# Attention, two mixture layers and a list scheduler on one core: sums and conversions of the attention stage put in another order and partly on another engine

## Chip, cores and metric

One core of one Trainium2 chip runs the whole program. The metric is the device time of one execution in microseconds; of the kernel before three runs were timed, and their median stands for it.

## The reference

Inputs are q, k and v of shape (4, 12, 448, 64), a cap of 30, and the weights of two layers. Cut to what matters:

```python
scores = cap * np.tanh(scale * q @ k.T / cap)
attn = np.exp(scores - max); attn = attn / attn.sum(-1)
x = (attn @ v).transpose(...).reshape(1792, 768)
# soft mixture of 8 experts with 4 slots each
logits = x @ phi                       # (1792, 32)
d = softmax(logits, over tokens); c = softmax(logits, over slots)
slot_out[e] = relu((d.T @ x)[e] @ w1[e]) @ w2[e]
x = c @ slot_out
# dense layer, 768 -> 2048 -> 768
y = (s * relu(x @ w_in) ** 2 + b) @ w_out
```

## The kernel before

The program has three stages. The **attention stage** goes over 24 pairs of heads (`NP`). Keys are cut into four chunks j = 0 to 3 of a pair n (three of 128 keys for both heads, and one in which the last 64 keys of both heads lie side by side). For each pair TensorE transposes q and k (`emit_tr`, L443), VectorE or ScalarE copies them out of PSUM (`emit_trc`, L410), TensorE makes the scores (`emit_qk`, L486), ScalarE takes tanh (L494) and exp (L508), and TensorE multiplies by v (`emit_av`, L529 and L534), which VectorE or ScalarE copies out to xu (`emit_avc`, L410). The row sums of exp are gathered in a tile es: `emit_es` (L516) adds the chunks 0 and 1, then chunk 2, in two additions over 128 x 896, and `emit_esl` (L521) adds chunk 3 in two additions over 64 x 448. Each two pairs, `emit_den` (L552) sums es over the partitions with a matrix of ones, into four groups of 32 output partitions, one for each head; for the last pair it takes chunks 2 and 3 straight from exp, so those two heads have three matmuls each. Then come the transposed denominators (`emit_row_t`, L565; `emit_rd`, L570 and L574), the logits (`emit_lg`, L580; `emit_lgw`, L588; `emit_lgr`, L597 to L606), the transposed outputs (`emit_xt`, L612; `emit_xtm`, L617), and after each six pairs a running softmax over tokens.

The weights `w_in` and `w_out` reach the program as 64-bit words. Twenty pieces of 768 KB are **converted** to 32-bit floats during the attention stage, where VectorE, GpSimd and ScalarE have room: SyncE loads the words (`cv_load`, L201), VectorE makes two passes (`conv_a`, L214 and L217), ScalarE one (`conv_f`, L224), VectorE or GpSimd adds the two parts (`conv_m`, L227), and SyncE stores the piece to a scratch area (`cv_store`, L334). The words have two buffers, w. SyncE also loads the experts' weights ahead (`load_next`, L356 and L362): ten pieces of w1, four of w2, and after the last conversion six more of w2, in buffers that the conversion had held.

The **expert stage** (L934 to L1003) is fed with the rest of the experts' weights as buffers of the attention stage come free. The **dense stage** (from L1055 on) loads the converted pieces and makes y.

The order of the attention stage isn't written by hand. `ListSchedule.run` takes all operations with an assumed duration on each engine that may do them, their needs, buffers (`acq`, `rel`) and a priority, and plays them forward in an assumed time: it takes the engine that can start first, and there the operation with the smallest priority among those that can start within 0.02. An operation with two engines goes to the one on which it ends first, with an extra charge for some (`DES`, `DESL`, `HACT`). What comes out is an order for each engine; the assumed times are not in the program. On the chip each engine goes through its list in order and waits at an instruction until its inputs are there. A result counts as there `lat` after its operation's end, 0.2 by default. Conversions have the priority `CV0 + CVP * i`, on a scale on which a pair of heads is 2, and none is loaded before `CVA`.

```python
PX, PA, DES, DESL, HACT = -0.32, 1.5, 4.98, 1.5, 0.96
CV0, CVP, CVA, WA = 9.33, 6.53, 20.19, 30.39
...
op(("cl", i), [(SP, 2.19)], cv_load, [], pr - 6, [("w", i)], lat=LAT, after=CVA)
op(("ca", i), [(DVE, 2.0)], cv_a, [("cl", i)], pr, [("cm", i), ("ce", i)], [("w", i)])
```

Of the kernel before, what the change touches and what calls it, by code (L numbers as in the profile page):

```python
# [28 lines left out]
ACT, DVE, POOL, PE, SP = "ACT", "DVE", "POOL", "PE", "SP"  # L29


class ListSchedule:

    def __init__(self, rings):
        self.bufs = rings
        self.ops = {}

    def add(self, name, engs, fn, need=(), prio=0.0, acq=(), rel=(), after=0.0, lat=0.2):

        self.ops[name] = dict(
            engs=engs, fn=fn, need=list(need), prio=prio, acq=acq, rel=rel, after=after, lat=lat
        )

    def run(self):
        end, free, freed, holds = {}, {}, {}, {}
        got = {r: [] for r in self.bufs}
        waits, after = {}, {}  # L50
        for name, o in self.ops.items():
            need = set(o["need"])
            waits[name] = len(need)
            for d in need:
                after.setdefault(d, []).append(name)
            for x in o["rel"]:
                holds[x] = holds.get(x, 0) + 1
        ready = [name for name, n in waits.items() if n == 0]
        while ready:
            best = {}  # L60
            for name in ready:
                o = self.ops[name]
                t = max([o["after"]] + [end[d] for d in o["need"]])
                for ring, _ in o["acq"]:
                    k = len(got[ring]) - self.bufs[ring]
                    if k >= 0:
                        t = max(t, freed.get((ring, got[ring][k]), 1e9))
                if t < 1e8:
                    _, t, eng, dur = min(
                        (max(t, free.get(e, 0.0)) + d + sum(x), max(t, free.get(e, 0.0)), e, d)  # L70
                        for e, d, *x in o["engs"]
                    )
                    best.setdefault(eng, []).append((t, o["prio"], name, dur))
            eng = min(best, key=lambda e: min(c[0] for c in best[e]))
            t0 = min(c[0] for c in best[eng])
            t0, _, name, dur = min((c for c in best[eng] if c[0] <= t0 + 0.02), key=lambda c: c[1])
            ready.remove(name)
            o = self.ops[name]
            free[eng] = t0 + dur
            end[name] = free[eng] + o["lat"]  # L80
            for ring, owner in o["acq"]:
                got[ring].append(owner)
            for x in o["rel"]:
                holds[x] -= 1
                if not holds[x]:
                    freed[x] = end[name]
            o["fn"](eng)
            for d in after.get(name, ()):
                waits[d] -= 1
                if not waits[d]:  # L90
                    ready.append(d)
        assert len(end) == len(self.ops)
# [3 lines left out]
def kernel(  # L96
# [16 lines left out]
    nc = tc.nc  # L113
    B, H, S, D = q.shape
# [25 lines left out]
    for j in range(3):  # L140
        blk = ident[32 * j:32 * j + 32, 32 * j:32 * j + 32]
        nc.scalar.copy(
            out=rep[32 * j:32 * j + 32],
# [142 lines left out]
    def run(safe):  # L286
        W1N, W2N = (4, (4,)) if safe else (10, (4, 6))
        NV, NEB, NEL, NES, NXU, NXQ, NQK = 2, 4, 2, 2, 4, 3, 2
        PX, PA, DES, DESL, HACT = -0.32, 1.5, 4.98, 1.5, 0.96
        CV0, CVP, CVA, WA = 9.33, 6.53, 20.19, 30.39  # L290

        PT, PDEN, PLG, PLW, PXT, PXM, PSO, PSL = -2.67, 1.0, 2.0, 3.4, 3.33, 2.05, 0.25, 4.75
        wctx = ExitStack()
# [76 lines left out]
        ones = c1_p.tile([128, 128], F32, name="ones")  # L370
# [22 lines left out]
        KC = S // 128  # L393
# [4 lines left out]
        spt, et, est, xut = {}, {}, {}, {}  # L398
# [4 lines left out]
        def tp(name):  # L403
            return ps_t.tile([128, 512], F32, tag="tp", name=name)
# [137 lines left out]

        def emit_den(g, _):
            pst["den", g] = ps = tp("dn")
            for j in range(4):
                n, h = 2 * g + j // 2, j % 2
                parts = [(slice(0, 128), est[n][:, h])]
                if n == NP - 1:
                    rows = slice(KL * h, KL * h + KL)
                    parts += [(slice(0, 128), et[n, KC - 1][:, h]), (rows, et[n, KC][rows, 0])]  # L550
                for i, (rows, x) in enumerate(parts):
                    nc.tensor.matmul(  # L552
                        out=ps[32 * j:32 * j + 32, 0:S], lhsT=ones[rows, 0:32], rhs=x,
                        start=(i == 0), stop=(i == len(parts) - 1),
                    )

        def emit_row_c(which, g, e):
            dnt[which, g] = t = sb_p.tile([128, S], F32, tag="dn", name="dn")
# [160 lines left out]
        ))  # L719

        def op(name, engs, f, need=(), prio=0.0, acq=(), rel=(), **kw):
            sch.add(name, engs, lambda e: f(*name[1:], e), need, prio, acq, rel, **kw)

        def cp(dve=True, hact=HACT):
            return [(DVE, 0.62)] * dve + [(ACT, 0.53, hact)]

        LAT = 2.0
        op(("const",), [(SP, 0.1)], load_const, prio=3.0, lat=LAT, after=2.0)
        for n in range(NP):
            f = 2 * n  # L730
            for w in "qk":
                i = ("ld", w, n)
# [3 lines left out]
            i = ("ld", "v", n)  # L736
# [8 lines left out]
            for j in range(KC + 1):  # L745
                u, m = f + j * 2 / (KC + 1), 1 if j < KC else 0.5
# [9 lines left out]
                rel = [(ring, (n, j))]  # L756
                if 0 < j < (KC if n < NP - 1 else KC - 1):
                    op(
                        ("es", n, j), [(POOL, 2.3), (DVE, 1.3, DES)], emit_es,
                        [("exp", n, j), ("exp", n, 0) if j == 1 else ("es", n, j - 1)], u + 1,  # L760
                        [("es", n)] if j == 1 else [], rel + [("e", (n, 0))] * (j == 1),
                    )
                if j == KC and n < NP - 1:
                    for h in range(2):
                        op(
                            ("esl", n, h), [(POOL, 1.2), (DVE, 0.68, DESL)], emit_esl, [("exp", n, j), ("es", n, j - 1)],
                            u + 1, [], rel,
                        )
                op(
                    ("av", n, j), [(PE, 0.85)], emit_av, [("exp", n, j), i] + [("av", n, j - 1)] * (j > 0), u + PA,  # L770
# [4 lines left out]
        for g in range(NQ):  # L775
            bb, gq = divmod(g, NQUAD)
            u0, last = 4 * g + 4, g == NQ - 1
# [3 lines left out]
            if last:  # L781
                es += [("es", NP - 1, KC - 2)] + [("exp", NP - 1, j) for j in (KC - 1, KC)]
                rel += [("e", (NP - 1, KC - 1)), ("el", (NP - 1, KC))]
            op(("den", g), [(PE, 0.82)], emit_den, es, u0 + PDEN, [("tp", ("den", g))], rel)
            if last:
                for j in range(2):
                    sch.add(
# [60 lines left out]
        need = []  # L848
        for i in range(len(cvs)):
            pr = CV0 + CVP * i  # L850
            op(("cl", i), [(SP, 2.19)], cv_load, [], pr - 6, [("w", i)], lat=LAT, after=CVA)
            op(("ca", i), [(DVE, 2.0)], cv_a, [("cl", i)], pr, [("cm", i), ("ce", i)], [("w", i)])
            op(("cf", i), [(ACT, 0.92)], cv_f, [("ca", i)], pr, [], [("w", i)])
            op(("cmul", i), [(DVE, 1.23), (POOL, 1.83)], cv_m, [("cf", i)], pr, [], [("ce", i)])
            op(("cst", i), [(SP, 1.1)], cv_store, [("cmul", i)], pr, [], [("cm", i)], lat=LAT)
            need = [("cst", j) for j in range(i + 1)]

# [488 lines left out]
```

## Time and profile before

| what | value |
|---|---|
| median of 3 runs | 662.75 us (657.78 to 663.97) |
| the profiled execution | 664.11 us |
| its span, first to last instruction | 662.3 us |
| mean granted TensorE clock | 0.959 |
| busy share: TensorE (PE), VectorE (DVE), ScalarE (ACT), GpSimd (POOL) | 92%, 56%, 60%, 30% |
| attention stage, expert stage, dense stage, about | 0 to 306, 306 to 380, 380 to 662 us |
| HBM traffic | 125.14 MB read, 13.37 MB written |

PE is the engine of matmuls, DVE is VectorE, ACT ScalarE, POOL GpSimd, SP SyncE with its DMA queue. A row of a timeline gives the start and the length of an instruction in us and, in brackets, how long its engine had been idle before it and which instruction ended that. In rows by stretch, an engine's number is its busy time in the stretch, in brackets its instructions; PEclk is the granted clock of TensorE (1.00 is 2.4 GHz, the lower level 0.50 is 1.2 GHz). "DMA share" is the mean busy share of the 16 DMA engines; it can read slightly over 1.

### The profile page before, as it was taken

What the parts mean: (1) busy time and instruction counts of PE and PEld (TensorE: products, weight loads), DVE (VectorE), ACT (ScalarE), POOL (GpSimd) and SP (SyncE); (2) the same over time, 40 slices, a digit from 0 to 9 for tenths busy, and PEclk for the clock granted to TensorE, in tenths of its full rate; (3) what the DMA queues carried; (4) which work ended last, traced back from release to release, by engine and by line L of the source; (5) the groups of instructions that cost most, each with busy time, mean ns of one, the idle gap of its engine ahead of it and who ended that gap; (6) DMA issues with size and microseconds to landing.
All of it is one profiled execution on the core that took longest, in us unless ns stands there. A gap on an engine that the chain in (4) does not pass through costs nothing.

```text
span 662.3 us, 10246 instructions
## 1 busy us (share of the span) xinstructions
PE 607.6 (92%) x3994; PEld 361.7 (55%) x3994; DVE 369.0 (56%) x518; ACT 396.5 (60%) x566; POOL 199.6 (30%) x116
## 2 busy tenths in 40 slices
PE   6979989889899999987985689999999999999995
PEld 3323333333233333333652368888888888888784
DVE  2397877768974445335460158992467669611221
ACT  4884876677666775720000188886666666656683
POOL 1694647576755555500000153421000000000000
PEclk9998989899999999996997789999999999999998
DMA  8675998979978531239999997340587779200201
GB/s 153 176 239 164 322 283 276 310 240 294 293 242 254 193 70 29 78 126 345 405 402 405 397 367 254 133 140 1 177 310 255 247 250 328 102 1 1 95 1 53
DMA packets 110345, 139.27 MB, mean 210 GB/s; under 512 B 52432, under 2 KB 84944, under 8 KB 110288
## 3 DMA queue, kind: packets, MB, share of 16 engines
q1 hardware_dynamic: 109344, 138.43, 63.6%
q8 instruction: 33, 0.54, 0.3%
q10 hardware_dynamic: 944, 0.10, 0.1%
q14 instruction: 24, 0.20, 0.1%
HBM read 125.14 MB, written 13.37 MB: 209 GB/s over the span
## 4 chain that ended last, share of the span: by engine, by line
PE 74%; DMA 12%; DVE 9%; ACT 2%; issue 1%; POOL 1%; SPq 0%; DVEq 0%; ACTq 0%; POOLq 0%
PE y L1197 23%; PE y L1198 12%; PE sp L486 10%; PE av L529 8%; DMA w2c<-in_moe_w_dram 5%; PE tr L443 3%; DMA w<-in_moe_w_out_dram 3%; PE av L534 2%; DVE cm L217 2%; PE h1p L946 2%; PE dn L552 2%; DVE cm L214 2%; PE xt L612 2%; PE gp L1129 2%; DMA w<-in_moe_w_in_dram 2%; DMA w<-scr 2%
## 5 line engine op out<-in xcount | busy, mean ns | idle before, releaser
L494 ACT ACTIVATE e<-sp,tsc 128x896 f32<-128x896 f32 x96 | 87.2, 911 | 78.9 <-PE sp L486 77.5
L1197 PE MATMUL y<-wo,gh 128*128 128x512 f32 x336 | 127.0, 400 | 0.0
L1174 DVE TENSOR_TENSOR gl<-r,gh 128x512 fp32r<-128x512 f32 (+1 forms) x65 | 44.5, 685 | 102.3 <-ACT r L1159 102.2
L486 PE MATMUL sp<-qs,ks 64*128 64x448 f32 (+1 forms) x384 | 98.4, 592 | 0.0
L1198 PE MATMUL y<-wo,gh 128*128 128x256 f32 x336 | 94.4, 281 | 0.0
L508 ACT ACTIVATE e<-e,capt 128x896 f32<-128x896 f32 x96 | 89.7, 946 | 1.8
L529 PE MATMUL av<-e,vn 128*64 128x448 f32 x288 | 74.0, 591 | 5.5 <-DVE xu L410 5.5
L516 POOL TENSOR_TENSOR es<-e 128x896 f32<-128x896 f32 x24 | 51.1, 2129 | 88.4 <-ACT e L508 55.0
L1146 ACT ACTIVATE r<-gp 128x512 f32<-128x512 f32 (+1 forms) x65 | 35.0, 539 | 60.8 <-PE gp L1129 59.3
L1197 PEld LDWEIGHTS y<-wo,gh 128*128 128x128 f32 x336 | 63.2, 188 | 13.8 <-issue 1.6
L1197 PE MATMUL y<-wo,gl 128*128 128x512 f32 x168 | 66.7, 397 | 0.0
L1198 PEld LDWEIGHTS y<-wo,gh 128*128 128x128 f32 x336 | 63.1, 188 | 1.7
L268 DVE TENSOR_REDUCE rng<-w 128x1 f32<-128x768 f32 x64 | 56.9, 944 | 0.0
L217 DVE SCALAR_TENSOR_TENSOR cm<-w,cm 128x768 int32<-128x768 int32 x32 | 53.3, 1664 | 1.1
L486 PEld LDWEIGHTS sp<-qs,ks 64*128 64x128 f32 (+1 forms) x384 | 28.1, 178 | 44.4 <-issue 24.1
L521 POOL TENSOR_TENSOR es<-es,e 64x448 f32<-64x448 f32 x35 | 49.3, 1410 | 8.4 <-ACT e L508 6.2
L516 POOL TENSOR_TENSOR es<-es,e 128x896 f32<-128x896 f32 x23 | 50.7, 2206 | 3.7 <-ACT e L508 2.7
L1159 ACT ACTIVATE r<-r,bt,st 128x512 f32<-128x512 f32 (+1 forms) x65 | 49.1, 756 | 1.8
L1159 ACT ACTIVATE gh<-r,bt,st 128x512 fp32r<-128x512 f32 (+1 forms) x65 | 49.1, 757 | 1.6
L1198 PE MATMUL y<-wo,gl 128*128 128x256 f32 x168 | 47.1, 281 | 0.0
L1197 PE MATMUL y<-woe,gh 128*128 128x512 f32 x112 | 44.3, 418 | 0.0
L214 DVE TENSOR_SCALAR cm<-w 128x768 int32<-128x768 int32 x32 | 35.4, 1107 | 15.5 <-DMA w<-in_moe_w_out_dram 8.4
(152 smaller groups left out, 907.8 us busy)
## 6 DMA issues: line engine op xcount, KB each, us to landing
w<-in_moe_w_in_dram SPq DMA_DIRECT2D x32, 768.0 KB, 5.8
w<-in_moe_w_out_dram SPq DMA_DIRECT2D x32, 768.0 KB, 6.1
w1c<-in_moe_w_dram SPq DMA_DIRECT2D x24, 1024.0 KB, 9.5
w2c<-in_moe_w_dram SPq DMA_DIRECT2D x26, 768.0 KB, 12.7
scr<-cm SPq DMA_DIRECT2D x20, 384.0 KB, 5.1
w<-scr SPq DMA_DIRECT2D x20, 384.0 KB, 5.9
qn<-in_q_dram SPq DMA_DIRECT2D x24, 224.0 KB, 4.1
kn<-in_k_dram SPq DMA_DIRECT2D x24, 192.0 KB, 4.3
```

The costliest lines, as they stand in the source:

```text
L214: nc.vector.tensor_scalar(out=m, in0=hi, scalar1=3, scalar2=0x3FFFFFF8, op0=ALU.logical_shift_left, op1=ALU.bitwise_and)
L217: nc.vector.scalar_tensor_tensor(out=m, in0=hi, scalar=-0x40000000, in1=m, op0=ALU.bitwise_and, op1=ALU.bitwise_or)
L268: nc.vector.tensor_reduce(out=rng[:, j, i:i + 1], in_=hi, axis=AX.X, op=o, apply_absolute_value=True)
L486: nc.tensor.matmul(out=sp[:, h, 0:S] if j < KC else sp[KL * h:KL * h + KL, 0, 0:S], lhsT=ks[n][rows, 128 * j:min(128 * j + 128, S)], rhs=q ...
L494: nc.scalar.activation(out=e, in_=spt.pop((n, j))[:, 0:m, 0:S], func=AF.Tanh, scale=tsc)
L508: nc.scalar.activation(out=e, in_=e, func=AF.Exp, scale=capt)
L516: eng.tensor_tensor(out=t, in0=et[n, 0] if j == 1 else t, in1=et[n, j], op=ALU.add)
L521: eng.tensor_tensor(out=t, in0=t, in1=et[n, KC][KL * h:KL * h + KL, 0], op=ALU.add)
L529: nc.tensor.matmul(out=out, lhsT=vt[n][:, KC * h + j, :], rhs=et[n, j][:, h], start=(j == 0), stop=False)
L1159: nc.scalar.activation(out=out, in_=in_, func=AF.Identity, scale=st, bias=bt)
L1197: nc.tensor.matmul(out=ya, lhsT=lhsT, rhs=w[:, 0:512], start=first, stop=last)
L1198: nc.tensor.matmul(out=yb, lhsT=lhsT, rhs=w[:, 512:768], start=False, stop=last and i0 == per - 1)
```

## The change

`ListSchedule` gets a new rule. Operations can be marked with `port=(DVE, POOL)`; among these, one doesn't start in the assumed time before the last marked one on either engine has ended. Marked are the es additions (`es`, `esl`) and the conversion's passes on DVE and POOL (`ca`, `cmul`). The extra charges for DVE fall (`DES` 4.98 to 1.0, `DESL` 1.5 to 0.5, `HACT` 0.96 to 0.5), the assumed durations of the marked operations are shorter, and the default `lat` is 0.6 instead of 0.2 for all of the stage's operations that go through `op` but qk, tanh and exp. Conversion i isn't loaded before `CVA + 9.5 * i`, its words are taken to need 3.0 instead of 2.0 to land, and conversions have an earlier priority (`CVP` 6.53 to 2.0). `emit_den` goes through the parts in the outer loop and the heads in the inner one; the last one's priority is later by 1.

```diff
+        def start(o, e, t):
+            return max(t, free.get(e, 0.0), port[0] if e in o["port"] else 0.0)
...
+            if eng in o["port"]:
+                port[0] = free[eng]
...
-        PX, PA, DES, DESL, HACT = -0.32, 1.5, 4.98, 1.5, 0.96
-        CV0, CVP, CVA, WA = 9.33, 6.53, 20.19, 30.39
+        PX, PA, DES, DESL, HACT = -0.32, 1.5, 1.0, 0.5, 0.5
+        CV0, CVP, CVA, CVT, WA = 9.33, 2.0, 20.19, 9.5, 30.39
+        LATE = 0.6
...
-                for i, (rows, x) in enumerate(parts):
-                    nc.tensor.matmul(
-                        out=ps[32 * j:32 * j + 32, 0:S], lhsT=ones[rows, 0:32], rhs=x,
-                        start=(i == 0), stop=(i == len(parts) - 1),
-                    )
+            for i in range(3):
+                for j in range(4):
+                    if i < len(parts[j]):
+                        rows, x = parts[j][i]
+                        nc.tensor.matmul(
+                            out=ps[32 * j:32 * j + 32, 0:S], lhsT=ones[rows, 0:32], rhs=x,
+                            start=(i == 0), stop=(i == len(parts[j]) - 1),
+                        )
...
+            kw = {"lat": LATE if name[0] not in ("qk", "tanh", "exp") else 0.2, **kw}
...
-                        ("es", n, j), [(POOL, 2.3), (DVE, 1.3, DES)], emit_es,
+                        ("es", n, j), [(POOL, 2.1), (DVE, 1.1, DES)], emit_es,
...
-                            ("esl", n, h), [(POOL, 1.2), (DVE, 0.68, DESL)], emit_esl, [("exp", n, j), ("es", n, j - 1)],
-                            u + 1, [], rel,
+                            ("esl", n, h), [(POOL, 1.13), (DVE, 0.63, DESL)], emit_esl, [("exp", n, j), ("es", n, j - 1)],
+                            u + 1, [], rel, port=BOTH,
...
-            op(("cl", i), [(SP, 2.19)], cv_load, [], pr - 6, [("w", i)], lat=LAT, after=CVA)
-            op(("ca", i), [(DVE, 2.0)], cv_a, [("cl", i)], pr, [("cm", i), ("ce", i)], [("w", i)])
+            op(("cl", i), [(SP, 2.19)], cv_load, [], pr - 6, [("w", i)], lat=3.0, after=CVA + CVT * i)
+            op(("ca", i), [(DVE, 1.55)], cv_a, [("cl", i)], pr, [("cm", i), ("ce", i)], [("w", i)], port=BOTH)
...
-            op(("cmul", i), [(DVE, 1.23), (POOL, 1.83)], cv_m, [("cf", i)], pr, [], [("ce", i)])
+            op(("cmul", i), [(DVE, 0.95), (POOL, 1.63)], cv_m, [("cf", i)], pr, [], [("ce", i)], port=BOTH)
```

The first place is on DVE, around pair 2 of heads. In the order before, L521 is an es addition of chunk 3, L214 and L217 are the conversion's first passes (here of the third piece, w_437), the three L410 copy xu, q and k out of PSUM.

```order
L521 TENSOR_TENSOR es<-es,e 64x448
L214 TENSOR_SCALAR cm<-w_437 128x768
L217 SCALAR_TENSOR_TENSOR cm<-w_437,cm 128x768
L410 COPY xu<-av 128x448
L410 COPY qs<-tr 128x448
L410 COPY ks<-tr 128x448
L588 TENSOR_TENSOR lw<-rowt,rd 112x512
L227 ISA cm<-cm,ce 128x1536
```

In the order now the same place reads (L524 is the es addition over 128 x 896, L529 that over 64 x 448, L418 the copies, L221 and L224 the conversion's passes, now of the second piece, w_430):

```order
L524 TENSOR_TENSOR es<-es,e 128x896
L582 TENSOR_SCALAR rd<-rowt 112x16
L586 RECIPROCAL rd<-rd 112x16
L529 TENSOR_TENSOR es<-es,e 64x448 x2
L418 COPY xu<-av 128x448
L600 TENSOR_TENSOR lw<-rowt,rd 112x512
L418 COPY qs<-tr 128x448
L418 COPY ks<-tr 128x448
L609 TENSOR_REDUCE lall<-lw 112x128
L629 TENSOR_TENSOR xq<-xt,rd 112x4x128 x2
L221 TENSOR_SCALAR cm<-w_430 128x768
L224 SCALAR_TENSOR_TENSOR cm<-w_430,cm 128x768
```

The conversion that stood ahead of the copy of xu now comes six instructions behind it, and three es additions stand ahead of that copy, where one stood (the other two were POOL's). Over the whole stage, of the 47 additions over 128 x 896 DVE does 16 now and none before; of the 46 over 64 x 448 it does 29 and before 11; of the 20 `conv_m` it does 17 and before 13.

The second place is the end of SP's list for the attention stage: the last six w2c pieces (L362) and the loads of v, q and k of the last pairs. In the order before:

```order
L362 DMA w2c<-in_moe_w_dram 128x2x768 x3
L429 DMA vn<-in_v_dram 128x2x192
L434 DMA vn<-in_v_dram 64x64 x2
L419 DMA qn<-in_q_dram 112x8x64
L424 DMA kn<-in_k_dram 128x6x64
L425 DMA kn<-in_k_dram 64x2x64
L362 DMA w2c<-in_moe_w_dram 128x2x768 x3
L429 DMA vn<-in_v_dram 128x2x192
```

In the order now, where L342 stores converted pieces and L364 begins the loads of the expert stage:

```order
L208 DMA w_2221<-in_moe_w_out_dram 128x1536
L342 DMA scr_116<-cm 128x768
L437 DMA vn<-in_v_dram 128x2x192
L442 DMA vn<-in_v_dram 64x64 x2
L342 DMA scr_117<-cm 128x768
L370 DMA w2c<-in_moe_w_dram 128x2x768
L437 DMA vn<-in_v_dram 128x2x192
L442 DMA vn<-in_v_dram 64x64 x2
L370 DMA w2c<-in_moe_w_dram 128x2x768 x5
L364 DMA w1c<-in_moe_w_dram 128x2x1024 x2
```

The last conversions reach to the last three pairs, and the six w2c stand directly ahead of the expert stage's loads, where before they stood five and six pairs earlier.

The third place is on PE, at the last sums. Before, L552 sums over partitions (es of a head, or chunks e), L529 and L534 multiply by v, L565 transposes:

```order
L552 MATMUL dn<-es,ones 32x448 x3
L552 MATMUL dn<-e,ones 32x448 x2
L552 MATMUL dn<-es,ones 32x448
L552 MATMUL dn<-e,ones 32x448 x2
L529 MATMUL av<-e,vn 64x448 x2
L565 MATMUL rowt<-ident,dn 112x128 x4
L534 MATMUL av<-e,vn 64x448 x2
```

Now:

```order
L564 MATMUL dn<-es,ones 32x448 x4
L564 MATMUL dn<-e,ones 32x448 x4
L537 MATMUL av<-e,vn 64x448 x2
L542 MATMUL av<-e,vn 64x448 x2
L577 MATMUL rowt<-ident,dn 112x128 x4
```

The four first parts stand side by side, then the two second parts and the two third parts; the transposes moved behind the last product with v.

## Rows read from the trace of the kernel before

**Rows 1.** Busy time by stretch, all engines: with conversions, without.

```profile
core 0: us, PE busy (x) PEld busy (x) DVE busy (x) ACT busy (x) POOL busy (x), PEclk, DMA share, GB/s
40.00:200.00 160.00, 144.44 (x742) 52.33 (x740) 126.42 (x152) 108.00 (x131) 103.64 (x58) 0.94 0.87 269
200.00:280.00 80.00, 80.00 (x432) 28.29 (x428) 36.29 (x65) 57.14 (x66) 42.56 (x26) 1.00 0.43 124
```

**Rows 2.** The same two stretches, score matmuls of L486 alone.

```profile
40.00:200.00 160.00, 50.31 (x200) 13.90 (x196) 0.94 0.87 269
200.00:280.00 80.00, 30.88 (x124) 8.67 (x124) 1.00 0.43 124
```

**Rows 3.** Who waited for whom, PE from 40 to 200 us: total, times, longest.

```profile
PE xt L612 <- DVE lw L588: 8.1, 3, 3.0
PE av L529 <- DVE xu L410: 5.5, 2, 4.6
```

**Rows 4.** Timeline of DVE, around 40 to 56 us.

```profile
40.70 5.20 DVE L214 TENSOR_SCALAR cm<-w 128x768 int32<-128x768 int32 x1
45.94 2.71 DVE L217 SCALAR_TENSOR_TENSOR cm<-w,cm 128x768 int32<-128x768 int32 x1
48.58 0.61 DVE L410 COPY xu<-av 128x448 f32<-128x448 f32 x1
...
55.03 0.55 DVE L214 TENSOR_SCALAR cm<-w 128x768 int32<-128x768 int32 x1
55.61 0.96 DVE L217 SCALAR_TENSOR_TENSOR cm<-w,cm 128x768 int32<-128x768 int32 x1
```

**Rows 5.** Timeline of POOL, the same stretch.

```profile
40.14 1.53 POOL L521 TENSOR_TENSOR es<-es,e 64x448 f32<-64x448 f32 x1
41.63 1.82 POOL L227 TENSOR_TENSOR cm<-cm,ce 128x768 int32<-128x768 int32 x1
43.42 2.07 POOL L516 TENSOR_TENSOR es<-e 128x896 f32<-128x896 f32 x1
45.56 2.28 POOL L516 TENSOR_TENSOR es<-es,e 128x896 f32<-128x896 f32 x1
...
59.87 2.08 POOL L516 TENSOR_TENSOR es<-e 128x896 f32<-128x896 f32 x1 [9.03 <-PE dn L552]
```

**Rows 6.** Timeline of PE, the same stretch.

```profile
49.24 3.25 PE L529 MATMUL av<-e,vn 128*64 128x448 f32 x8 [4.57 <-DVE xu L410]
```

**Rows 7.** Groups by line and shape, 0 to 302 us: busy, mean ns, idle before.

```profile
L217 DVE SCALAR_TENSOR_TENSOR cm<-w,cm 128x768 int32<-128x768 int32 x20 | 35.5, 1777 | 0.7
L214 DVE TENSOR_SCALAR cm<-w 128x768 int32<-128x768 int32 x20 | 24.4, 1219 | 15.3 <-DMA w<-in_moe_w_out_dram 8.4 <-DMA w<-in_moe_w_in_dram 6.9
L521 POOL TENSOR_TENSOR es<-es,e 64x448 f32<-64x448 f32 x35 | 49.3, 1410 | 8.4 <-ACT e L508 6.2 <-PE sl L689 0.4
```

**Rows 8.** Timeline of DVE, one addition of chunk 3.

```profile
266.24 0.62 DVE L521 TENSOR_TENSOR es<-es,e 64x448 f32<-64x448 f32 x1 [0.28 <-ACT e L508]
```

**Rows 9.** Timeline of PE, the last sums.

```profile
286.20 0.95 PE L552 MATMUL dn<-es,ones 128*32 128x448 f32 x6
286.99 1.78 PE L552 MATMUL dn<-e,ones 128*32 128x448 f32 x4
288.70 0.94 PE L552 MATMUL dn<-es,ones 128*32 128x448 f32 x2
289.48 1.78 PE L552 MATMUL dn<-e,ones 128*32 128x448 f32 x4
```

**Rows 10.** Busy time by stretch, all engines, columns as in rows 1.

```profile
270.00:280.00 10.00, 10.00 (x52) 3.00 (x52) 2.30 (x5) 7.64 (x10) 6.45 (x4) 1.00 0.42 129
280.00:290.00 10.00, 10.00 (x46) 3.27 (x44) 3.80 (x6) 3.91 (x5) 2.10 (x1) 1.00 0.32 105
290.00:300.00 10.00, 6.71 (x34) 2.79 (x32) 3.63 (x7) 1.60 (x3) 0.45 (x1) 1.00 0.52 184
...
330.00:340.00 10.00, 9.45 (x196) 6.28 (x192) 7.47 (x12) 0.00 (x0) 0.00 (x0) 1.00 1.04 404
```

More of the change, by code (lines that the diff above doesn't have):

```diff
@@ L39, in __init__, with add @@
         self.ops = {}
-    def add(self, name, engs, fn, need=(), prio=0.0, acq=(), rel=(), after=0.0, lat=0.2):
+    def add(self, name, engs, fn, need=(), prio=0.0, acq=(), rel=(), after=0.0, lat=0.2, port=()):
         self.ops[name] = dict(
-            engs=engs, fn=fn, need=list(need), prio=prio, acq=acq, rel=rel, after=after, lat=lat
+            engs=engs, fn=fn, need=list(need), prio=prio, acq=acq, rel=rel, after=after, lat=lat, port=port
         )
@@ L48, in run @@
         end, free, freed, holds = {}, {}, {}, {}
+        port = [0.0]
         got = {r: [] for r in self.bufs}
@@ L69, in run @@
                     _, t, eng, dur = min(
-                        (max(t, free.get(e, 0.0)) + d + sum(x), max(t, free.get(e, 0.0)), e, d)
-                        for e, d, *x in o["engs"]
+                        (start(o, e, t) + d + sum(x), start(o, e, t), e, d) for e, d, *x in o["engs"]
                     )
@@ L544, in emit_den @@
             pst["den", g] = ps = tp("dn")
+            parts = []
             for j in range(4):
                 n, h = 2 * g + j // 2, j % 2
-                parts = [(slice(0, 128), est[n][:, h])]
+                parts.append([(slice(0, 128), est[n][:, h])])
                 if n == NP - 1:
                     rows = slice(KL * h, KL * h + KL)
-                    parts += [(slice(0, 128), et[n, KC - 1][:, h]), (rows, et[n, KC][rows, 0])]
-                for i, (rows, x) in enumerate(parts):
-                    nc.tensor.matmul(
-                        out=ps[32 * j:32 * j + 32, 0:S], lhsT=ones[rows, 0:32], rhs=x,
-                        start=(i == 0), stop=(i == len(parts) - 1),
-                    )
+                    parts[j] += [(slice(0, 128), et[n, KC - 1][:, h]), (rows, et[n, KC][rows, 0])]
+            for i in range(3):
[6 more added lines that the diff above has]
+                        )
         def emit_row_c(which, g, e):
@@ L727, in run @@
         LAT = 2.0
+        BOTH = (DVE, POOL)
         op(("const",), [(SP, 0.1)], load_const, prio=3.0, lat=LAT, after=2.0)
@@ L758, in run @@
                     op(
-                        ("es", n, j), [(POOL, 2.3), (DVE, 1.3, DES)], emit_es,
+                        ("es", n, j), [(POOL, 2.1), (DVE, 1.1, DES)], emit_es,
                         [("exp", n, j), ("exp", n, 0) if j == 1 else ("es", n, j - 1)], u + 1,
-                        [("es", n)] if j == 1 else [], rel + [("e", (n, 0))] * (j == 1),
+                        [("es", n)] if j == 1 else [], rel + [("e", (n, 0))] * (j == 1), port=BOTH,
                     )
@@ L783, in run @@
                 rel += [("e", (NP - 1, KC - 1)), ("el", (NP - 1, KC))]
-            op(("den", g), [(PE, 0.82)], emit_den, es, u0 + PDEN, [("tp", ("den", g))], rel)
+            op(("den", g), [(PE, 2.4 if last else 0.82)], emit_den, es, u0 + PDEN + last, [("tp", ("den", g))], rel)
             if last:
```

## Prediction

> **What bounds the kernel now.** I read the busy time by stretch first, then the waits, then the timelines of the engines in those waits. In the attention stage TensorE (PE) sets the pace. Where no conversions run, from 200 to 280 us, PE is busy for all of 80 us at the full granted clock; from 40 to 200 us, where nearly all conversions lie, it is busy for 144.44 of 160 us at a mean clock of 0.94 [rows 1]. So PE stands still for 15.6 us there, and at 0.94 of the clock another 160 x 0.06 = 9.6 us of work are lost, call it 9 because part of the slow time was idle: together some 25 us. A second reading bears this out: without conversions 124 score matmuls took 80 us, 0.645 us each; with them 200 took 160 us, 0.80 each, and 200 x 0.155 = 31 us [rows 2]. This is the same loss, with a few us of other work that falls unevenly; I use 25 and keep 31 as its upper bound.
>
> Whom does PE wait for? VectorE (DVE): its copy of xu and the product lw [rows 3], although DVE is only busy for 126 of those 160 us [rows 1]. The longest wait, 4.57 us, ends at 49.24, when the copy of xu is made [rows 6]. On DVE that copy stands behind two conversion passes of 5.20 and 2.71 us; where GpSimd (POOL) is idle the same two took 0.55 and 0.96 [rows 4]. POOL was idle there, for 9.03 us before 59.87, and in the slow place it did four additions, one right behind the other [rows 5]. Over the stage the two passes took 24.4 and 35.5 us for 20 pieces; at the undisturbed times they would be 11.0 and 19.2, so 29.7 us of DVE's time went into standing beside POOL [rows 7]. On top DVE stood idle for 15.3 us at the first pass, until the words had landed [rows 7], with the PSUM copies queued behind it.
>
> The Trainium skill, page SBUF — State Buffer, section "SBUF: two separate sides", says that VectorE and GpSimd share one pair of SBUF ports, which goes to whoever starts first for one whole instruction, while the other is blocked; a VectorE operation with two SBUF inputs counts too. The trace agrees that it blocks, but not on how long: the 5.20 us pass outlasted three GpSimd instructions and ended only during the fourth, where by the rule it would have gone after the first, at about 41.7, and would have lost about 1 us. By the page one meeting costs at most one GpSimd instruction, by the trace several in a row, so where runs of them get rarer the loss falls faster than GpSimd's busy time. By the rule alone the loss in part 2 below would only fall with that busy time, by 12.5 us, and the sum would end at 648 instead of 645. The rule also speaks against the change, since additions moved to VectorE now hold the pair themselves and stop GpSimd; no row here has GpSimd as the engine that PE waits for.
>
> **The change part by part.**
>
> 1. Additions leave POOL for DVE. DVE gets 16 over 128 x 896, 18 over 64 x 448 and 4 of the conversion's additions. A 64 x 448 addition took 0.62 us on DVE [rows 8]. Twice the columns take between 0.62 and 1.24; I take 1.15, near twice. The conversion's addition isn't among the rows for DVE; it has the columns of the second pass, so I take that pass's 0.96 [rows 4], between 0.55 and 1.9. This makes 18.4 + 11.2 + 3.8 = 33 us more for DVE. POOL gives up 16 x 2.08 [rows 5] + 18 x 1.41 [rows 7] + 4 x 1.82 [rows 5] = 66 us of the 146 that it was busy from 40 to 280 [rows 1]. The 33 us lie in DVE's idle time (34 of 160 us and 44 of 80 us in rows 1), and if all 29.7 us beside POOL went, DVE would be hardly busier than before. I cost them at nothing; without that cover each addition ahead of a copy delays it by 0.6 to 1.15 us, and DVE's waits for POOL's half of a sum come on top (the third rival).
>
> 2. Additions and conversions kept apart. Nothing on the chip keeps them apart; only the order does, as far as its assumed times hold. But even if they met by accident, POOL would be busy for about 80 of 240 us, 33%, instead of 65% (104 of 160 us in rows 1), so the losses beside it about halve. That separation which survives, and the next part, take more.
>
> 3. Conversions at even distances. Before, a load could go as soon as one of the two word buffers was free; now each has a time of its own, 9.5 after the last, the words are taken to need 3.0 instead of 2.0 to land, and more of PE's work stands between a load and its first pass. The 15.3 us of idle DVE can go to nothing, or grow, since the weight loads that fill SP's gaps come earlier and the DMA share was already 0.87 [rows 1]. The last seven or so conversions reach into the stretch that had no gaps. Parts 2 and 3 together are worth between minus 10 (a loss: new gaps in the late part, priced as seven conversions at 25 / 20 = 1.25 us each) and 31 us (rows 2); I take 15 of the 25, half by POOL's lower load and a little more for the distances.
>
> 4. The last sums. They took from 286.20 to 291.26 us, 5.06 us [rows 9]. The first three heads' first parts ran side by side in 0.79 us; then two matmuls into one group of output partitions took 1.71, 0.855 each, the fourth head's first part stood alone, and two more followed. Now there are three rounds, 0.79 + 2 x 0.855 = 2.5 us, so 2.5 us go; the bounds are 0 (if the sums or what follows then wait for a late addition or copy) and 2.5. The last head's PE work lies on the path to the expert stage, so I take 2.3.
>
> 5. The six w2c pieces come last on SP, after the last conversion's store. At 404 GB/s [rows 10] a piece of 768 KB takes 1.95 us, six 11.7. In the place where they now stand the DMA share was 0.42, 0.32 and 0.52 for 10 us each, so 17.4 us of the queue are free [rows 10]; the expert stage behind it is bound by DMA (1.04 in rows 10). I cost them at nothing; if they slide into the expert stage, at 11.7.
>
> The expert stage's loads wait for buffers of the attention stage, and neither it nor the dense stage has an instruction moved; so what the attention stage gains reaches the end. The sum against the profiled execution: 664.1 - 15 - 2.3 = 646.8. That execution lay 1.4 above the median of the runs, so the predicted median is 645.4, which I round up to 646.
>
> **The rivals.**
>
> *The stalls only move.* The order knows assumed times alone; DVE's additions now have two SBUF inputs in 45 places instead of 11, and the DMA share may keep the words late. Each conversion goes on costing 1.25 us and only the last sums gain: 662.75 - 2.3 = 660.5. For it: PE never waits for POOL's sums as such, only for DVE, and DVE gets more work. Against it: DVE's excess came from POOL's load, which falls by nearly half.
>
> *The w2c pieces slide into the expert stage.* All else as forecast: 645.4 + 11.7 = 657. For it: they follow the last store in an SP queue that goes in order. Against it: 17.4 us of room.
>
> *Slower: DVE waits for POOL in the middle of a sum.* In 12 of the 24 pairs POOL adds chunks 0 and 1 and DVE adds chunk 2 to that result; before, POOL did both, and DVE waited at most for chunk 3's part. DVE's queue stands still there, with the copies of xu, q and k behind it. Such a wait is between 0 and POOL's 2.08 us [rows 5]; with 1.0 us of it reaching PE and the clock's cost of 9 us shared over the five or so gaps, 1.9 each, it costs 12 x 2.9 = 35 us and gives 645.4 + 35 = 680, if it struck each time. It makes the kernel slower by 1% when it takes back 17.3 + 6.6 = 24 us, that is 2.0 us a pair. Against it: additions of chunk 2 follow those of chunk 1 on POOL anyway, and scores, not sums, are what PE needs next.
>
> **How the numbers follow.** Forecast (most of the loss goes): 0.69, from 636 (all 25 and the 2.3 go) to 656. Stalls only move: 0.17. w2c slide: 0.04. DVE waits for POOL: 0.10, of which 0.08 slower by over 1%. A measurement of this kernel tells about 1% from no change, 6.6 us. Faster by over 1% (under 656.1): 0.69. Within 1%: 0.17 + 0.04 + 0.02 = 0.23. Slower: 0.08. The range, 637 to 662, leaves out a complete recovery and the slower cases.
>
> **What would show each step.** Right: PE's waits for DVE's xu and lw under 8 us in the stage; the first pass's mean near 0.7 us and the second's near 1.2; POOL's busy time about 66 us lower; the last sums in 2.5 us; the expert stage beginning near 289 instead of about 306 us. Wrong: DVE idle until the words land for more than 15 us again, DVE waiting for an es addition of POOL with PE waiting for the copy behind it, the clock at half speed after 200 us, or w2c still moving when the expert stage begins.

## The result, and the profile after

The changed kernel takes 639.28 us (median of 4 runs, 638.24 to 640.40), the kernel before beside it 661.95: a ratio of 0.967, with a 95% interval of 0.963 to 0.971. The forecast was 646, its range 637 to 662. Direction and cause held; the gain is 22.7 us where about 17 was worked out. The profiled execution took 640.16 us, its span 638.4.

The busy time by stretch, the columns as in [rows 1]:

```profile
40.00:200.00 160.00, 159.55 (x866) 58.16 (x862) 122.14 (x181) 125.63 (x151) 58.62 (x35) 1.00 0.86 258
200.00:280.00 80.00, 74.54 (x410) 26.77 (x412) 54.91 (x87) 52.11 (x66) 30.14 (x17) 1.00 0.66 218
```

Between 40 and 200 us PE is idle for 0.45 us instead of 15.56, and its granted clock is 1.00 instead of 0.94: the whole of the 25 us came back, not 15 of it. Most of the 5.5 idle us of the second stretch lie after 270, where the attention stage now ends. GpSimd's busy time in the first stretch fell from 103.64 to 58.62 us, and VectorE has no more than before (122 instead of 126), with the sums that it took over. Whom PE waited for from 7 to 290 us (total, times, longest; the rows that answer to [rows 3] are those for lw of L600 and for xu):

```profile
...
PE ltp L642 <- DVE lw L615: 1.8, 1, 1.8
PE tr L451 <- DMA qn<-in_q_dram: 1.7, 2, 1.4
PE tr L451 <- DMA kn<-in_k_dram: 0.8, 1, 0.8
PE xt L624 <- DVE lw L600: 0.7, 1, 0.7
...
PE av L537 <- DVE xu L418: 0.5, 1, 0.5
```

The 13.6 us of [rows 3] are down to 1.2. The groups of VectorE in the attention stage, as in [rows 7], with one of the kernel before that isn't shown there (its additions of chunk 3) at the end:

```profile
L224 DVE SCALAR_TENSOR_TENSOR cm<-w,cm 128x768 int32<-128x768 int32 x20 | 26.9, 1347 | 0.7
L529 DVE TENSOR_TENSOR es<-es,e 64x448 f32<-64x448 f32 x29 | 18.4, 636 | 1.9 <-POOL es L524 1.2
L221 DVE TENSOR_SCALAR cm<-w 128x768 int32<-128x768 int32 x20 | 15.5, 776 | 8.7 <-DMA w<-in_moe_w_in_dram 4.9 <-DMA w<-in_moe_w_out_dram 3.7
L524 DVE TENSOR_TENSOR es<-es,e 128x896 f32<-128x896 f32 x12 | 13.0, 1086 | 3.6 <-POOL es L524 2.3 <-ACT e L516 1.3
...
L521 DVE TENSOR_TENSOR es<-es,e 64x448 f32<-64x448 f32 x11 | 7.9, 720 | 6.6 <-POOL es L516 5.6 <-ACT e L508 0.8
```

The two passes are shorter, 776 ns instead of 1219 and 1347 instead of 1777, but far from the undisturbed 0.55 and 0.96 us of [rows 4]: (0.776 - 0.55 + 1.347 - 0.96) x 20 = 12 us of stretching are left of 29.7, and 8.7 us of waiting for words of 15.3. PE feels next to nothing of either. An addition over 128 x 896 takes 1.09 us on VectorE, half of GpSimd's 2.08. VectorE waited for GpSimd's half of a sum for 2.3 + 1.2 = 3.5 us in the whole stage; in the kernel before it had done so for 5.6, a third cause of its lateness beside the passes and the words.

One meeting of the two engines, on VectorE, with an undisturbed pass below it:

```profile
36.63 2.73 DVE L224 SCALAR_TENSOR_TENSOR cm<-w,cm 128x768 int32<-128x768 int32 x1
...
52.81 0.96 DVE L224 SCALAR_TENSOR_TENSOR cm<-w,cm 128x768 int32<-128x768 int32 x1
```

and what GpSimd did then:

```profile
36.23 2.31 POOL L524 TENSOR_TENSOR es<-e 128x896 f32<-128x896 f32 x1 [6.49 <-ACT e L516]
```

GpSimd's addition ends at 38.54, with nothing behind it, and the pass 0.82 us later, at 39.36: it was held by one instruction and then ran at about its own 0.96.

The last sums, on PE, as in [rows 9]:

```profile
266.71 0.96 PE L564 MATMUL dn<-es,ones 128*32 128x448 f32 x8
267.50 1.79 PE L564 MATMUL dn<-e,ones 128*32 128x448 f32 x8
```

From 266.71 to 269.29 they take 2.58 us instead of 5.06. The six w2c pieces, of which five are issued one right behind the other (issues on SP, 253 to 257 us, with the median time to landing; then the stretch, columns as before):

```profile
w2c<-in_moe_w_dram SPq DMA_DIRECT2D x5, 768.0 KB, 8.7
...
255.00:270.00 15.00, 15.00 (x78) 4.85 (x76) 7.58 (x12) 8.31 (x10) 1.50 (x2) 1.00 1.02 388
```

The pieces fill the queue from 255 to 270 us (DMA share 1.02, where [rows 10] have 0.32 to 0.52 for 10 us each), and the last of them lands at 267.5, 16 us ahead of the expert stage. Its first matmul starts at 284.0 instead of 307.3. The first matmuls by w2c:

```profile
314.12 2.12 PE L967 MATMUL so<-w2c,h1m 128*32 128x192 f32 x48
...
290.77 2.77 PE L981 MATMUL so<-w2c,h1m 128*32 128x192 f32 x64
```

They come 6.8 us after the stage's first matmul in both kernels, the second line's being the changed one, PE waits 6.3 us for w2c in the stage in both, and the first matmul of y (L1203, before L1189) comes 75.0 us after the stage's first, where it was 74.8: nothing slid.

Along the stage the difference stands as follows: the second pair's tanh begins 4.5 us later than before (a loss that nobody expected), from there to the last pair 24.0 us are won, from there to the expert stage 3.8: 24.0 + 3.8 - 4.5 = 23.3, the same as 307.3 - 284.0. The place of the loss on PE:

```profile
13.15 0.58 PE L451 MATMUL tr<-ident,qn 112*128 112x112 f32 x4 [1.43 <-DMA qn<-in_q_dram]
14.49 1.17 PE L451 MATMUL tr<-ident,kn 128*128 128x128 f32 x4 [0.77 <-DMA kn<-in_k_dram]
15.31 3.64 PE L494 MATMUL sp<-qs,ks 64*128 64x448 f32 x8
```

PE waits for q and k of the third pair, and from 14.2 to 21.0 us the granted clock is 0.5, the lower of its two levels (1.2 GHz), after full speed from 10.8: eight score matmuls take 3.64 us here and 1.97 in the kernel before, which had no wait at this place. Its row, and those of the loads around it, before and after (start, time to issue):

```profile
14.01 1.97 PE L486 MATMUL sp<-qs,ks 64*128 64x448 f32 x8
8.81 0.63 SPq L419 DMA_DIRECT2D qn<-in_q_dram  x1
11.12 1.45 ACTq L707 DMA_DIRECT2D phibd<-in_moe_phi_dram  x2
...
8.80 0.63 SPq L427 DMA_DIRECT2D qn<-in_q_dram  x1
8.21 1.45 ACTq L719 DMA_DIRECT2D phibd<-in_moe_phi_dram  x2
```

SP issues q and k of the third pair at the same times in both kernels, behind the same loads. What moved is phi, two loads on ScalarE's queue: they are issued 2.9 us earlier, the first of them now ahead of q, and q lands at 13.0 instead of 12.3 us, k at 14.4 instead of 13.3. A second trace of the changed kernel (the run after_again below) has the same waits, 1.29 and 0.74 us; there the lower clock lasts from 14.5 to 17.9 us only, the second pair's tanh begins 3.0 us later than in the kernel before and the expert stage at 282.3. So the size of this loss differs from execution to execution.

### The profile page after: what moved, and what is told of

The parts are those of the page before. It is cut to its first block, busy times and chain, and to the rows that moved or that the text cites. A ratio compares the mean times of both kernels' runs of the same rounds, so it can differ in the third digit from the quotient of the medians.

```text
span 638.4 us, 10213 instructions
## 1 busy us (share of the span) xinstructions
PE 597.1 (94%) x3994; PEld 358.7 (56%) x3994; DVE 372.3 (58%) x547; ACT 399.8 (63%) x575; POOL 129.2 (20%) x78
## 4 chain that ended last, share of the span: by engine, by line
PE 83%; DMA 10%; DVE 3%; ACT 1%; issue 0%; SPq 0%; ACTq 0%
PE y L1211 25%; PE sp L494 13%; PE y L1212 12%; PE av L537 9%; DMA w2c<-in_moe_w_dram 5%; PE tr L451 4%; PE av L542 3%; PE h1p L960 2%; PE gp L1143 2%; DMA w<-in_moe_w_out_dram 2%; PE xt L624 2%; PE dn L564 2%; DMA w<-scr 2%; PE rowt L577 2%; PE lg L592 1%; PE so L981 1%
## 5 line engine op out<-in xcount | busy, mean ns | idle before, releaser
L1188 DVE TENSOR_TENSOR gl<-r,gh 128x512 fp32r<-128x512 f32 (+1 forms) x65 | 42.4, 653 | 102.9 <-ACT r L1173 102.8
L537 PE MATMUL av<-e,vn 128*64 128x448 f32 x288 | 71.1, 568 | 0.6 <-DVE xu L418 0.5
L524 POOL TENSOR_TENSOR es<-e 128x896 f32<-128x896 f32 x20 | 42.1, 2106 | 109.9 <-ACT e L516 55.0
L224 DVE SCALAR_TENSOR_TENSOR cm<-w,cm 128x768 int32<-128x768 int32 x32 | 44.7, 1396 | 1.1
L1098 ACT CAST woe<-w 128x768 fp32r<-128x768 f32 x2 | 1.7, 830 | 67.0 <-PE gp L1112 67.0
L1167 ACT ACTIVATE r<-r 128x512 f32<-128x512 f32 (+1 forms) x65 | 37.1, 573 | 1.7
L537 PEld LDWEIGHTS av<-e,vn 128*64 128x64 f32 x288 | 15.0, 136 | 38.0 <-issue 27.2
```

The source lines that it names most:

```text
L224: nc.vector.scalar_tensor_tensor(out=m, in0=hi, scalar=-0x40000000, in1=m, op0=ALU.bitwise_and, op1=ALU.bitwise_or)
L524: eng.tensor_tensor(out=t, in0=et[n, 0] if j == 1 else t, in1=et[n, j], op=ALU.add)
L537: nc.tensor.matmul(out=out, lhsT=vt[n][:, KC * h + j, :], rhs=et[n, j][:, h], start=(j == 0), stop=False)
L1167: nc.scalar.activation(out=t, in_=t, func=AF.Square)
L1188: eng.tensor_tensor(out=gl, in0=t, in1=f32(gh), op=ALU.subtract)
```

## Experiments on the order before

Three kernels keep the order before, instruction by instruction, and take away one disturbance each or both: GpSimd's hold on the ports, by additions over 16 columns only (with a memset for the rest of es), and the late words, by loading only the first two pieces. The short additions also end earlier, so short_pool and neither take away VectorE's waits for GpSimd's half of a sum, 5.6 us before, as well; these runs don't tell them from the hold on the ports.

```diff
# short_pool, and neither; esl and conv_m are cut on GpSimd in the same way
+            w = 16 if e == POOL else S
+            if w < S and j == 1:
+                eng.memset(t[:, :, w:S], 1.0)
             eng.tensor_tensor(
-                out=t, in0=et[n, 0] if j == 1 else t, in1=et[n, j], op=ALU.add)
+                out=t[:, :, 0:w], in0=(et[n, 0] if j == 1 else t)[:, :, 0:w], in1=et[n, j][:, :, 0:w], op=ALU.add)
# no_words, and neither
-            env[i] = load_words(i, c_p)
+            env["w", i] = env[i] = load_words(i, c_p) if i < 2 else env["w", i - 2]
```

> The order of the kernel before, unchanged; GpSimd's additions in the attention stage take 16 columns instead of all (a memset fills the rest of es), so the row sums and some converted weights are left out of the computation. Theory P (VectorE's passes are stretched beside GpSimd, and PE's gaps and slow clock from 40 to 200 us follow from that): the first pass falls from 1.22 to about 0.6 us, the second from 1.78 to about 1.0, and most of the 25 us goes: 642 to 648 us. Theory W (the words land too late for the bunched conversions, and VectorE waits for them with the copies queued behind): VectorE still waits 15 us for words, the gaps stay, 657 to 662 us. If each has its part, about 650 to 656.

> The order of the kernel before; 18 of the 20 word loads are left out, each conversion takes the words of the first or second piece again, so the converted weights are not the reference's. GpSimd and VectorE do all they did. Theory P: the passes stay at 1.2 and 1.8 us, the gaps stay, 655 to 662 us. Theory W: VectorE waits for no words, most of the gaps go, 640 to 650 us.

> Both of the former at once (the same parts of the computation left out). Theories P and W together: no gap over 1 us and no slow clock from 40 to 200 us, so 662 - 25 = 637 us or a little less. If gaps of more than 8 us in all stay, the cause is neither, and is the order itself (a copy behind an instruction that waits for something else).

Against 661.62 us for the kernel before in these runs, short_pool took 645.07 (ratio 0.978, 0.973 to 0.982), no_words 649.85 (0.983, 0.979 to 0.986), neither 637.53 (0.965, 0.961 to 0.968). The first stretch of short_pool, columns as in [rows 1]:

```profile
40.00:200.00 160.00, 156.31 (x850) 57.04 (x848) 102.08 (x169) 123.20 (x147) 34.82 (x77) 1.00 1.00 308
```

its passes on VectorE:

```profile
L217 DVE SCALAR_TENSOR_TENSOR cm<-w,cm 128x768 int32<-128x768 int32 x20 | 19.3, 963 | 0.7
L214 DVE TENSOR_SCALAR cm<-w 128x768 int32<-128x768 int32 x20 | 12.4, 619 | 31.4 <-DMA w<-in_moe_w_out_dram 13.7 <-DMA w<-in_moe_w_in_dram 13.6 <-DMA scr<-cm 4.1
```

The first stretch of no_words:

```profile
40.00:200.00 160.00, 152.53 (x808) 54.97 (x806) 135.99 (x164) 117.89 (x141) 112.69 (x62) 0.99 0.66 202
```

its passes:

```profile
L217 DVE SCALAR_TENSOR_TENSOR cm<-w,cm 128x768 int32<-128x768 int32 x20 | 39.7, 1987 | 0.7
L214 DVE TENSOR_SCALAR cm<-w 128x768 int32<-128x768 int32 x20 | 23.0, 1148 | 1.5 <-DMA w<-in_moe_w_in_dram 1.4
```

and the first stretch of neither:

```profile
40.00:200.00 160.00, 160.00 (x868) 58.33 (x868) 103.79 (x169) 125.82 (x151) 37.86 (x78) 1.00 0.73 223
```

Both disturbances are real: without GpSimd's long additions 16.6 us go, without the late words 11.8 (their intervals touch, so which is larger isn't shown), without both 24.1, and then PE has no gap at all in this stretch. What surprised is how each gain comes. (The profiled execution of short_pool, at 640.93 us, is the fastest of its four, 4.1 us below their median, so its rows show less loss than most of its executions had.) In short_pool VectorE waits for words twice as long as before (31.4 us instead of 15.3), and yet PE is idle for only 3.7. In no_words the passes are as stretched as ever (1148 and 1987 ns), and yet half of PE's idle time is gone (7.5 us instead of 15.6). So PE's loss isn't in proportion to what VectorE loses. A reading that fits: PE has other matmuls whose inputs are there, and only what a disturbance takes beyond them reaches it, so with one of the two away, much of the other no longer does. The sum of the single gains, 28.3, lies above the joint one, 24.1, as that would have it, but with intervals of 2.3 to 2.9 us either way on each gain the difference isn't clear of noise, and the work that PE has ahead of it was measured in no run.

**The last sums alone.** The new `emit_den` in the kernel before, and nothing else:

```diff
-                for i, (rows, x) in enumerate(parts):
+            for i in range(3):
+                for j in range(4):
...
```

> The kernel before with the parts of the last sums side by side, nothing else. Both theories: the sums in 2.5 instead of 5.0 us, and 2.3 us less, 659.5 us; 0 if a copy or an addition is late next.

Measured: 658.83 us, ratio 0.997 (0.994 to 0.999), 2.8 us less. On PE the sums take 2.58 us, exactly as in the changed kernel:

```profile
284.17 0.96 PE L556 MATMUL dn<-es,ones 128*32 128x448 f32 x8
284.96 1.79 PE L556 MATMUL dn<-e,ones 128*32 128x448 f32 x8
```

## Experiments on the order now

**One part undone at a time.** No marked operations; no even distances; the old charges for VectorE, with which GpSimd gets the sums back:

```diff
# no_port_rule
-        BOTH = (DVE, POOL)
+        BOTH = ()
# bunched
-        CV0, CVP, CVA, CVT, WA = 9.33, 2.0, 20.19, 9.5, 30.39
+        CV0, CVP, CVA, CVT, WA = 9.33, 6.53, 20.19, 0.0, 30.39
-            op(("cl", i), [(SP, 2.19)], cv_load, [], pr - 6, [("w", i)], lat=3.0, after=CVA + CVT * i)
+            op(("cl", i), [(SP, 2.19)], cv_load, [], pr - 6, [("w", i)], lat=LAT, after=CVA + CVT * i)
# old_charges
-        PX, PA, DES, DESL, HACT = -0.32, 1.5, 1.0, 0.5, 0.5
+        PX, PA, DES, DESL, HACT = -0.32, 1.5, 4.98, 1.5, 0.96
```

> The changed kernel, planned without the rule that keeps the marked operations of the two engines apart; charges, latencies and distances as changed, so the planner is free to give GpSimd more again. Theory P, with the rule as its main part: the passes go back above 1.0 and 1.5 us, 650 us or more. Theory W, or P by GpSimd's lower load alone: 638 to 644 us.

> The changed kernel with the conversions' priorities, loads and landing time of the kernel before (no distances). Theory W: VectorE waits 15 us or more for words, 650 us or more. Theory P: the passes stay near 0.8 and 1.3 us, 638 to 644 us.

> The changed kernel with the old extra charges for VectorE (4.98, 1.5 and 0.96), so GpSimd keeps most sums; the rule for the ports, the distances and the latencies stay. Theory P by GpSimd's load: the passes are stretched again, 650 us or more. If the rule alone can keep them apart, or theory W holds: 638 to 644 us.

Measured, against 662.01 us for the kernel before: no_port_rule 648.4 (ratio 0.978, 0.973 to 0.984), bunched 642.62 (0.972, 0.967 to 0.976), old_charges 645.22 (0.974, 0.969 to 0.979). The first clearly loses against the changed kernel, some 9 us, and seemed to show that keeping the additions apart is what counts. But without the rule the list also divides the sums otherwise: GpSimd got 17 more of them, 65 of the 93 instead of 48 (the expectation for no_rule_same_engines below says 16). Its first stretch, and that of old_charges below it:

```profile
40.00:200.00 160.00, 157.82 (x843) 56.77 (x841) 118.15 (x161) 121.43 (x148) 83.02 (x48) 0.99 0.86 253
```

```profile
40.00:200.00 160.00, 150.38 (x814) 56.07 (x816) 114.75 (x159) 109.06 (x131) 100.17 (x58) 0.98 0.84 249
```

In the first GpSimd is busy for 83.02 us instead of 58.62, and PE is idle for 2.2; its longest wait, 3.5 us at 239 us, lies behind this stretch. In the second GpSimd has all 93 sums, and nearly the load of [rows 1]; PE is idle for 9.6 us, yet 17 of the 23 us stay won. So fewer sums on GpSimd aren't the only thing that helps. Of the 17 us the new last sums bring 2.8 (above); the rest comes, at the old load, from the rule, the distances, the earlier priority, the assumed durations and the latency together. Which of them does it there wasn't tried.

**The rule alone, the division held.** To separate order from division, the next kernel drops the rule, but gives every sum and conversion addition the engine it has in the changed kernel. (The PSUM copies aren't held: VectorE makes 67 of the 96 here, 75 in the changed kernel and 84 in the one before.) Another one undoes the longer assumed latency; the changed kernel and bunched ran again beside them.

```diff
# no_rule_same_engines; the tables list the engine of each operation
+            if name[0] in ("es", "esl", "cmul") and not safe:
+                dve = name in on_dve if name[0] == "es" else name not in on_pool
+                engs = [x for x in engs if (x[0] == DVE) == dve]
...
-        BOTH = (DVE, POOL)
+        BOTH = ()
# lat_0_2
-        LATE = 0.6
+        LATE = 0.2
```

> The changed kernel planned without the port rule, but with every sum and conversion addition held on the engine that it has in the changed kernel, so only the order differs. Planning without the rule cost 9 us, with 16 more additions on GpSimd. If that came from GpSimd's load: 639 to 641 us here. If the order that the rule makes is what counts: 645 us or more.

> The changed kernel planned with the old default latency of 0.2 instead of 0.6, all else as changed. If the longer assumed latency is part of the gain (it sets producers further ahead of PE's use): 642 us or more. Theories P and W give it no part: 638 to 640 us.

> The changed kernel itself once more, beside the next three on one chip, so that they can be compared with it: 639 us, within 1.

> The changed kernel with the conversions bunched again, timed in more rounds. If the distances are worth something by themselves once the sums are divided: 642 to 644 us, clear of the changed kernel. If not: 639 to 640 us.

Measured, against 660.87 us: no_rule_same_engines 640.21 (ratio 0.968, 0.964 to 0.971), lat_0_2 639.9 (0.968, 0.965 to 0.972), the changed kernel 639.4 (0.968, 0.964 to 0.971), bunched 643.51 (0.973, 0.968 to 0.978). The first stretch of no_rule_same_engines:

```profile
40.00:200.00 160.00, 160.00 (x865) 57.86 (x864) 126.71 (x173) 128.21 (x160) 63.32 (x36) 1.00 0.89 260
```

No gap at all, and the same time as the changed kernel. With the division of the sums held, the order that the rule makes is worth nothing that can be measured: what its removal cost in no_port_rule came with the 17 sums that went back to GpSimd. At GpSimd's old load the rule alone wasn't tried.

The whole time also holds the unforeseen loss at the start, which differs between these kernels. The timelines of ScalarE give the stretch without it, from the second pair's first tanh to the last pair's, in one trace each (two for the changed kernel and for bunched):

| kernel | second pair's tanh begins | from there to the last pair's |
|---|---|---|
| before | 19.3 us | 255.2 us |
| changed | 23.8, 22.3 | 231.2, 230.4 |
| no_port_rule | 22.4 | 241.6 |
| old_charges | 20.5 | 239.1 |
| bunched | 20.6, 20.7 | 234.9, 235.4 |
| lat_0_2 | 19.5 | 234.1 |
| no_rule_same_engines | 20.5 | 231.6 |

Here too the order made by the rule is worth nothing clear. The longer latency isn't worth nothing in itself: lat_0_2 has no loss at the start, where its phi is issued at 11.1 us as in the kernel before, and loses 3 to 4 us later, so that the two cancel in the whole time. The even distances came out at 3.3 and 4.1 us in the two sets of runs, both times in the same direction, and the table has 4 to 5; the intervals of the ratios overlap, so as a gain of the whole kernel that stays open.

**The start.** This kernel undoes the unforeseen loss: v of pair 1 is loaded only after k of pair 2, and the two small loads of `st` and `bt` only after q of pair 4.

```diff
+        held = {}
+
+        def load(which, n, e):
+            if (which, n) == ("v", 1):
+                held["k", 2] = lambda: load_now("v", 1, e)
+                return
+            load_now(which, n, e)
+            held.pop((which, n), lambda: None)()
...
                 for t, src in ((st, s), (bt, b)):
+                    held["q", 4] = lambda: load_sb()
```

> The changed kernel with only the order of SP's first loads changed: q and k of the third pair ahead of v of the second, and the two small constants later. In the changed kernel PE waited 1.43 and 0.77 us for q and k there, and ran at half the granted clock from 14.2 to 21.0 us. If that wait is what drops the clock, the waits go, the clock holds and about 1.5 to 4.5 us go: 635 to 638 us. If the clock at the start has a course of its own, about 1 us goes: 638 to 639 us.

Measured: 636.55 us, ratio 0.962 (0.959 to 0.966), against 662.01. On PE, at the place shown above:

```profile
12.33 1.01 PE L460 MATMUL tr<-ident,qn 112*128 112x112 f32 x4
13.13 0.88 PE L460 MATMUL tr<-ident,kn 128*128 128x128 f32 x4
13.74 1.97 PE L503 MATMUL sp<-qs,ks 64*128 64x448 f32 x8
```

The waits are gone, the eight score matmuls take 1.97 us again, and the clock doesn't fall. The second pair's tanh begins at 19.6 us instead of 23.8 (22.3 in the second trace), the expert stage at 280.4 instead of 284.0 (282.3), and from the second pair to the last there are 231.1 us, as in the changed kernel: what is won is won at the start. The median is 2.7 us below the changed kernel's; the intervals of the two ratios overlap, but five of its six runs lie below all ten of the changed kernel. So having q and k earlier removes the loss. That phi brought it about is the reading that fits: in all seven traces here with phi issued at 8.05 to 8.33 us and this order of loads PE waits for q and k of the third pair, for 0.8 to 2.2 us together; in those of the kernel before and of lat_0_2, with 11.1, it doesn't. Moving phi alone wasn't tried.

## Why the prediction was right, and where it was off

*What bounds the kernel.* Right: PE's 25 us were lost to VectorE's lateness, and VectorE's to GpSimd and late words. The two single removals and the joint one show both causes, and 24.1 us for both. With the ports went VectorE's waits for GpSimd's sums, 5.6 us before, which the prediction left out; their share isn't separated.

*Part 1, the additions that move.* Right at nothing. Up to the expert stage's first matmul GpSimd's busy time fell by 71 us (168.66 to 98.02) where 66 was worked out, an addition over 128 x 896 took 1.09 us where 1.15 was taken, and VectorE's busy time grew by only 4 (191.12 to 195.08) instead of 33, since its passes got 17 us shorter and nine PSUM copies of about 0.62 us went to ScalarE, which the prediction didn't count. (`HACT` is an extra charge on ScalarE's copies, not on VectorE as the section on the change has it; lowering it gives copies away.)

*Parts 2 and 3, apart and at even distances.* Here lies the miss: 15 of the 25 us were taken, and all 25 came. The step that failed is "so the losses beside it about halve". VectorE's stretching did fall by somewhat more than half (29.7 to 12 us) and its wait for words by nearly half (15.3 to 8.7). But this was then taken as PE's share, as if PE lost in proportion. It doesn't: 12 us of stretching and 8.7 of waiting for words are left, and PE's idle time from 40 to 200 us is 0.45 us instead of 15.56, with the clock back at 1.00. That short_pool and no_words each gave back more than a proportional share goes the same way. Why the rest doesn't reach PE is argued and not shown: it may lie within the work that PE has ahead, or the conversions may just stand behind the copies that PE waits for, as at the first place in the change. The wording of part 2, that its order would add to the gain beyond the load, isn't borne out: with the division of the sums held it adds nothing. And GpSimd's load was compared over unlike stretches there, 65% of 160 us with 33% of 240; over the same 240 us it was 61% and became 37%.

*The ports.* The Trainium skill, page SBUF — State Buffer, section "SBUF: two separate sides", gives the pair to one side for one whole instruction. The pass at 36.63 agrees, held by a single addition. The pass of 5.20 us in [rows 4] doesn't: it outlasted three that stood back to back [rows 5]. Both readings are needed, and the measurement decides. By the rule alone the sum was 648; the time came out below either sum, and that tells nothing between them, since the share of PE was off in both.

*Part 4, the last sums.* Right: 2.5 us were worked out and 2.3 taken; 2.48 in the trace, 2.8 by themselves.

*Part 5, w2c.* Right at nothing: the first matmul by w2c comes 6.8 us after the expert stage's first in both kernels, and PE's wait for w2c there is 6.3 us in both.

*Not foreseen, and luck.* 4.5 us lost at the start in one trace and 3.0 in another, where q and k land later; the prediction put the start at nothing without looking at it. Without this loss the time is 636.55 us, just below the range of 637 to 662, which left out a complete recovery. So that the number fell within the range is in part luck: a gain taken too small and a loss not seen at all worked against each other.

*The rivals.* The stalls didn't just move: PE's idle time went. The w2c pieces didn't slide. VectorE did wait for GpSimd in the middle of a sum, but for 3.5 us in all, less than the 5.6 of the kernel before, where the prediction had such waits at chunk 3's part at most; PE's longest waits for xu and lw are 0.5 and 0.7 us. The pairs in which GpSimd begins a sum and VectorE goes on are 11, not 12: in pair 4 VectorE does both.

## What to carry to other kernels

What a disturbed engine loses needn't be what the engine behind it loses, and not in proportion: here about half of VectorE's lateness stayed and nearly all of PE's went. So price a disturbance at the engine that sets the pace, by how late its inputs come, and let the range include that halving the disturbance wins everything. Where a list schedule has a rule for when things run, test it with the engines held fixed: the rule may work only through which engine it gives the work to. After any change of costs in such a list, look at the first twenty microseconds too, on every queue that loads: here a load on another queue moved. And compare kernels stretch by stretch: lat_0_2 and the changed kernel are equal in the whole time because a gain at the start cancels a loss behind it.

## What the runs showed of the hardware

- GpSimd's additions, one right behind the other, held a pass on VectorE through three of them (5.20 us instead of 0.55, [rows 4, 5]); a lone one held it only for itself (2.73 us, of which 1.91 are wait). With additions over 16 columns the two passes took 0.62 and 0.96 us on average instead of 1.22 and 1.78.
- Two short waits of PE, 1.43 and 0.77 us, soon after the clock had risen, were followed by the lower clock for 6.8 us and cost more than they lasted: 4.5 us at the second pair's tanh. In another execution 1.29 and 0.74 us were followed by 3.4 us of it and cost 3.0. Without them it stayed at full speed, and with 0.58 and 0.75 us (bunched, its second trace) too.
